# A new issue order in an attention and maxout-FFN kernel, with the loads of later batches as pieces of their own

## The chip, the core and the metric

The kernel runs on one core of one Trainium2 chip. A core has TensorE (PE, matmuls), VectorE (DVE), ScalarE (ACT), GpSimd (POOL) and SyncE (SP), each with an instruction stream of its own that it works off in order, and 16 DMA engines that all streams share. The metric is the device time of one execution in microseconds: before, the median of 3 runs is 178.24 us (178.22 to 178.28).

## The reference

Eight batches, 8 heads, a sequence of 576, head dimension 64, 32 memory slots. `phi` is turned into weights over the sequence, K and V are summed into 32 slots with them, and q attends to the slots. The result, 4608 tokens of 512 values, goes through a feed-forward network whose hidden layer is the maximum of three products.

```python
# _attn_ref (cut)
a = np.exp(phi - np.max(phi, axis=2, keepdims=True))
a = a / (np.sum(a, axis=2, keepdims=True) + 1e-09)
k_m = np.einsum('bhsm,bhsd->bhmd', a, k)
v_m = np.einsum('bhsm,bhsd->bhmd', a, v)
scores = scale * np.matmul(q, k_m.transpose(0, 1, 3, 2))
attn = softmax(scores)              # cut: max, exp, divide by the sum
out = np.matmul(attn, v_m)          # (8, 8, 576, 64)
# reference (cut): tokens x (heads * head_dim) = 4608 x 512
h = np.maximum(np.maximum(x @ w1, x @ w2), x @ w3)     # 512 -> 768
return h @ w_out                                       # 768 -> 512
```

## The kernel before

The kernel never forms `x`. As `attn @ v_m @ w` is `attn @ (v_m @ w)`, it folds the weights into the 32 slots of each head of a batch (D), and takes all hidden values straight from `attn`. It also uses max(a, b, c) = c + max(a - c, b - c, 0): `w1` and `w2` are replaced by their differences to `w3` (V), the relu and the max take the rest, and the part of `w3` goes around the hidden layer as `w3 @ w_out` (W and O).

The work is cut into pieces with one letter each, and the kernel is a list of them; `B@3` is piece B of batch 3. The order in the list is the order on every engine, as the schedule is manual. In the loop `+` and `-` after a name move it to a later or an earlier batch.

| piece | what it does | engines |
|---|---|---|
| E | exp of phi | ACT |
| B | sums of K and V (72 matmuls of 192 columns) | PE |
| N, K | divide by the sum of phi's exps; transpose (to `kvt`) | DVE; PE, then a DVE copy |
| Q0, Q1 | transpose q in 32x32 blocks, half each | DVE |
| S, M, R, X | scores and their exp; sums; reciprocal as exp(-ln); product `attn` | PE, ACT; PE; ACT; DVE |
| W, O, V | transpose w3, w3 @ w_out, differences of the weights (batch 0 alone) | PE, DVE; PE, ACT; DVE |
| D0 to D3 | fold `kvt` into the weights, evacuate to `wp` | PE, then ACT or DVE |
| F0 to F11 | a hidden tile: even ones end in a relu, odd ones in a max | PE, then ACT (even) or DVE (odd) |
| T0 to T4 | an output tile of 128 tokens and its store (T4 only in odd batches) | PE, then ACT or DVE, SP |
| Z24 | 24 matmuls on a zero tile | PE |

The loads are issued on GpSimd's queue. The buffers hold two batches, so the load of a batch needs the buffer of the batch two before it to be free. The first 14 are issued ahead of all pieces; each later one directly behind the last piece that reads its buffer:

```python
inp = ctx.enter_context(tc.tile_pool(name="inp", bufs=2))     # ph, qq
acc_pool = ... name="accp", bufs=3, space=PSUM                # tag "acc": B, S, M, D, F
one_pool = ... name="onep", bufs=2, space=PSUM                # tag "one": Z, W, O, K, T
# ...
load_ph(0)
load_kv(0)
load_q(0)
ident = const.tile([P, P], BF16, name="ident")
make_identity(nc, ident)
load_w(2)
nc.gpsimd.dma_start(out=wo_sb, in_=moe_w_out.rearrange("(t p) c -> p t c", p=P))
load_w(0)
load_w(1)
load_ph(1)
load_kv(1)
load_q(1)
# ...
EVAC = {"D": "aasa", "T": "vaavv"}     # a: ACT, v: DVE, s: half each
# ...
loads = ((load_ph, "E"), (load_kv, "B"), (load_q, "Q0 Q1"))

def done(b, n):
    issued.add((b, n))
    for f, names in loads:
        names = names.split()
        if n in names and b + 2 < B and all((b, m) in issued for m in names):
            f(b + 2)
# ...
issue(0, "Z24")
att_exp(0, halves[0])
att_exp(0, halves[1])
done(0, "E")
att_kv(0, range(0, NP // 2))
issue(0, "Z9")
att_kv(0, range(NP // 2, NP))
done(0, "B")
run(0, "N Z9 K Q0 Q1 S W0 W1 M0 R0 W2 M1 R1 V0")
# ... a list of pieces for batches 0 to 2 and the first ones of batch 3, then:
for b in range(2, B - 1):
    run(b, "T4- F6 F0 F7 F2 F1 F8 F10 F4 F9 F3 T2- S+ B++ N++ D3+ Q0++ E+++ T3- M0+")
    run(b, "R0+ F5 F11 M1+ X0+ R1+ T0 X1+ K++ D2+ D0+ D1+ T1 Q1++")
```

The weights w1, w2, w3 are `load_w(0)`, `load_w(1)`, `load_w(2)`, called w0, w1 and w2 below; `wo` is `moe_w_out`. V0 needs w2 and w0. V1 has two halves, of which the second needs w1; V2 needs w1. D0, D1, D2 need V0, V1, V2. k3 is the load of K of batch 3, and so on.

Of the kernel before, what the change touches and what calls it, by code (L numbers as in the profile page):

```python
# [15 lines left out]
def kernel(  # L16
# [12 lines left out]
    nc = tc.nc  # L29

    B, H, S, D = q.shape
    M = phi.shape[-1]
    P = 128
    NP = H // 2
# [36 lines left out]
    wo_sb = const.tile([P, FT, DM], BF16, name="wo_sb")  # L71
# [5 lines left out]
    def by_pair(src, b):  # L77
        return src[b].rearrange("h s d -> (h s) d").rearrange(
            "(j p c) d -> p j (c d)", p=P, c=NC
        )  # L80

    halves = [slice(0, NP // 2), slice(NP // 2, NP)]
# [11 lines left out]
    def load_kv(b):  # L94
        kv = kvos[b % 2]
        loaded.setdefault(b, {})["kv"] = kv
        for h in halves if b == 0 else [slice(0, NP)]:
            for i, src in enumerate((k, v)):
                nc.gpsimd.dma_start(  # L99
                    out=kv[:, i].rearrange("p j c d -> p j (c d)")[:, h],  # L100
                    in_=by_pair(src, b)[:, h],
                )

    def load_q(b):
        qq = inp.tile([P, NP, NC, D], BF16, name="qq")
        loaded.setdefault(b, {})["q"] = qq
        nc.gpsimd.dma_start(  # L107
            out=qq.rearrange("p j c d -> p j (c d)"), in_=by_pair(q, b)
        )

    def load_w(i):
        w = (moe_w1, moe_w2, moe_w3)[i]
        nc.gpsimd.dma_start(
            out=w_sb[:, :, i], in_=w.rearrange("(j p) f -> p j f", p=P)
        )

    load_ph(0)
    load_kv(0)
    load_q(0)
    ident = const.tile([P, P], BF16, name="ident")  # L120
    make_identity(nc, ident)
    load_w(2)
    nc.gpsimd.dma_start(out=wo_sb, in_=moe_w_out.rearrange("(t p) c -> p t c", p=P))
    load_w(0)
    load_w(1)
    load_ph(1)
# [18 lines left out]
            )  # L145


    EVAC = {"D": "aasa", "T": "vaavv"}

    def evacuate(kind, n, out_, in_):  # L150
        e = EVAC[kind][n]
        if e == "s":
            nc.scalar.copy(out=out_[:, 0], in_=in_[:, 0])
            nc.vector.tensor_copy(out=out_[:, 1], in_=in_[:, 1])
        elif e == "a":
            nc.scalar.copy(out=out_, in_=in_)  # L156
        else:
            nc.vector.tensor_copy(out=out_, in_=in_)  # L158
# [45 lines left out]
    def att_exp(b, js=slice(0, NP)):  # L204
        s = st.setdefault(b, {})
        if "e" not in s:
            s["e"] = work.tile([P, NP, NC, M], BF16, name="e")
        nc.scalar.activation(out=s["e"][:, js], in_=loaded[b]["ph"][:, js], func=AF.Exp)  # L208

    def att_kv(b, js=range(NP)):  # L210
        s = st[b]
        if "kvp" not in s:
            s["kvp"] = acc_pool.tile([P, NG, BANK], FP32, name="kvp", tag="acc")
        kv, kvp = loaded[b]["kv"], s["kvp"]
        for c in range(NC):
            for j in js:
                for a in range(NG):
                    r = slice(HP * a, HP * (a + 1))
                    nc.tensor.matmul(  # L219
                        kvp[M * j : M * (j + 1), a, 0 : 3 * D],  # L220
                        lhsT=s["e"][r, j, c, :],
                        rhs=kv[r, :, j, c, :],
                        start=(c == 0),
                        stop=(c == NC - 1),
                        tile_position=(HP * a, M * j),
                    )

    def att_kv_norm(b):

        s = st[b]  # L230
        kvp = s["kvp"]
        rden = work.tile([P, NG], FP32, name="rden")
        nc.vector.reciprocal(out=rden, in_=kvp[:, :, 2 * D])  # L233
        kvn = work.tile([P, 3, P], BF16, name="kvn")
        nc.vector.tensor_tensor(
            out=kvn[:, 0].rearrange("p (a d) -> p a d", a=NG),
            in0=kvp[:, :, D : 2 * D],
            in1=rden.unsqueeze(2).to_broadcast([P, NG, D]),
            op=ALU.mult,
        )  # L240
        for g in range(NG):
            kn = kvn[:, 1:3, HP * g : HP * (g + 1)]
            nc.vector.tensor_scalar_mul(
                out=kn.rearrange("p h (t d) -> p h t d", t=2),
                in0=kvp[:, g, 0:D]
                .rearrange("p (h d) -> p h d", h=2)
                .unsqueeze(2)
                .to_broadcast([P, 2, 2, R]),
                scalar1=rden[:, g : g + 1],
            )  # L250
        s["kvn"] = kvn

    def att_kv_t(b):


        s = st[b]
        ps = one_pool.tile([P, 3, P], BF16, name="kvtp", tag="one")
        for n in range(3):
            nc.tensor.transpose(ps[:, n], s["kvn"][:, n], ident)
        kvt = work.tile([P, 3, P], BF16, name="kvt")  # L260
        nc.vector.tensor_copy(out=kvt, in_=ps)
        s["kvt"] = kvt

    def att_q(b, n):


        s = st.setdefault(b, {})
        if "qT" not in s:
            s["qT"] = work.tile([P, NP, NC, 2, R], BF16, name="qT")
        j = halves[n]  # L270
        nc.vector.transpose(  # L271
            out=s["qT"][:, j].rearrange("p j c h r -> p (j c h r)"),
            in_=loaded[b]["q"][:, j].rearrange("p j c d -> p (j c d)"),
        )
# [34 lines left out]
    def att_sum(b, g):  # L309
        s = st[b]  # L310
        e2 = s["e2"]
        sm = acc_pool.tile([P, 2, BANK], FP32, name="sm", tag="acc")
        for h in range(2):
            nc.tensor.matmul(  # L314
                sm[:, h, 0:SH],
                lhsT=blkones,
                rhs=e2[:, g, h * SH : (h + 1) * SH],
                start=True,
                stop=True,
            )  # L320
        s["sm", g] = sm
# [126 lines left out]
            nc.sync.dma_start(out=rows[:, h[1]], in_=ot[:, h[1]])  # L448


    issued = set()
    loads = ((load_ph, "E"), (load_kv, "B"), (load_q, "Q0 Q1"))

    def issue(b, n):

        if not 0 <= b < B or (n == "T4" and b % 2 == 0):
            return
        i = int(n[1:]) if len(n) > 1 else None
        {
            "E": lambda: att_exp(b),  # L460
            "B": lambda: att_kv(b),
            "N": lambda: att_kv_norm(b),
            "K": lambda: att_kv_t(b),
            "Q": lambda: att_q(b, i),
            "S": lambda: att_score(b),
            "M": lambda: att_sum(b, i),
            "R": lambda: att_rec(b, i),
            "X": lambda: att_mul(b, i),
            "D": lambda: fold(b, i),
            "F": lambda: ffn1(b, i),  # L470
            "T": lambda: ffn2(b, i),
            "W": lambda: w3_t(i),
            "O": lambda: w3_o(i),
            "V": lambda: w_diff(i),
            "Z": lambda: warm_up(i),
        }[n[0]]()
        done(b, n)

    def done(b, n):
        issued.add((b, n))  # L480
        for f, names in loads:
            names = names.split()
            if n in names and b + 2 < B and all((b, m) in issued for m in names):
                f(b + 2)

    def run(b, text):

        for w in text.split():
            issue(b + w.count("+") - w.count("-"), w.rstrip("+-"))

    issue(0, "Z24")
    att_exp(0, halves[0])
    att_exp(0, halves[1])
    done(0, "E")
    att_kv(0, range(0, NP // 2))
    issue(0, "Z9")
    att_kv(0, range(NP // 2, NP))
    done(0, "B")
    run(0, "N Z9 K Q0 Q1 S W0 W1 M0 R0 W2 M1 R1 V0")
    for w in """  # L500
        O2@0 X1@0 O1@0 X0@0 O3@0 D0@0 O0@0 V1@0 F6@0 F0@0 V2@0 F2@0 D1@0 D2@0 F1@0 F4@0 F7@0
        F3@0 E@1 F5@0 F10@0 F8@0 F11@0 B@1 N@1 D3@0 F9@0 K@1 D0@1 Q0@1 E@2 Q1@1 T3@0 D2@1
        S@1 T1@0 M0@1 M1@1 T0@0 R1@1 R0@1 D3@1 X1@1 D1@1 X0@1 B@2 N@2 T2@0 F2@1 F6@1 F8@1
        Q0@2 Q1@2 F7@1 F0@1 K@2 F3@1 E@3 F1@1 F9@1 F4@1 F10@1 S@2 F5@1 F11@1 M1@2 B@3 R1@2
        D3@2 N@3 T0@1 Q0@3 X1@2 M0@2 E@4 R0@2 T1@1 D1@2 D0@2 D2@2 X0@2 Q1@3 K@3
    """.split():
        n, b = w.split("@")
        issue(int(b), n)
    for b in range(2, B - 1):
        run(b, "T4- F6 F0 F7 F2 F1 F8 F10 F4 F9 F3 T2- S+ B++ N++ D3+ Q0++ E+++ T3- M0+")  # L510
        run(b, "R0+ F5 F11 M1+ X0+ R1+ T0 X1+ K++ D2+ D0+ D1+ T1 Q1++")
    run(B - 1, "T4- F6 T2- F10 F2 F7 F8 F11 F0 F4 F1 F5 F9 F3 T3- T0 T4 T2 T3")
    ffn2(B - 1, 1, last=True)


# [28 lines left out]
```

The softmax here doesn't subtract the row's maximum and nothing guards it: scores larger than these inputs give would overflow.

## Time and profile before

| | before |
|---|---|
| time, median of 3 | 178.24 us |
| span of the profiled execution | 177.6 us |
| PE busy | 159.8 us |
| ACT busy, DVE busy | 105.9 us, 104.5 us |
| bytes read from HBM, written | 39.32 MB, 9.44 MB |
| loads on GpSimd's queue, issue to landing | 16 to 21 us (medians by tensor, from batch 1 on and the weights) |
| F, T, D on PE: matmuls | 384, 216 + 64 + 16, 256 |

Busy time counts the time in which an engine has an instruction in work, and PE's matmuls are pipelined, so a busy PE is not PE at its peak. The page has the span in 40 equal slices, with the busy share of each engine in tenths; it tells in which stage an engine is full. The chain of work that ended last names, from the end backwards, what each step waited for. "Issue to landing" is the time from a load's issue on GpSimd to its completion, and holds its time in the queue as well. Lines in the profile are lines of the kernel: L99 the loads of K and V, L107 those of q, L92 those of phi, L219 B, L358 D, L383 the matmuls of F, L393 and L395 its relu and max, L411, L420 and L429 the matmuls of T, L271 Q, L338 X, L191 V.

### The profile page before, as it was taken

To read this page: it belongs to the slowest core of one execution; us is meant where nothing else is said; L and a number is where in the kernel's file an instruction comes from. 1 tells how busy PE (TensorE), PEld (TensorE's weight loads), DVE (VectorE), ACT (ScalarE), POOL (GpSimd) and SP (SyncE) were. 2 spreads that over 40 slices of the span, in tenths; PEclk is the share of its full clock that TensorE was granted. 3 is DMA by queue.
4 is the path that set the end of the run, shared out by engine and by line. 5 is a ranking of instruction groups with operands and counts; after the bars stand their busy time and mean duration, and the time that the engine had idled before them with its cause. 6 is when DMAs were issued, how large, how long until landed. Compare 5 with 4: busy or idle time off the path is not lost.

```text
span 177.6 us, 4447 instructions
## 1 busy us (share of the span) xinstructions
PE 159.8 (90%) x1914; PEld 89.0 (50%) x1914; DVE 104.5 (59%) x164; ACT 105.9 (60%) x158; POOL 28.3 (16%) x43
## 2 busy tenths in 40 slices
PE   7895897788996596999999999999999999999990
PEld 2352634453564342755565547456664565466440
DVE  6407418679379366749855965597479553717420
ACT  4100467857885686659867767679477558872010
POOL 7951112043133050104013010000000000000000
PEclk9999699999999999999999999999999999999999
DMA  5999999999999999999999999213013201330333
GB/s 154 160 206 209 207 210 275 208 261 222 236 320 237 275 208 241 289 235 298 235 260 277 230 270 188 98 59 118 0 63 122 111 9 69 114 118 0 122 118 120
DMA packets 21973, 31.76 MB, mean 179 GB/s; under 512 B 1216, under 2 KB 16576, under 8 KB 21952
## 3 DMA queue, kind: packets, MB, share of 16 engines
q0 software_dynamic: 16080, 21.43, 63.4%
q1 hardware_dynamic: 5728, 9.90, 15.7%
q8 instruction: 15, 0.25, 0.5%
q10 hardware_dynamic: 144, 0.13, 0.2%
q14 instruction: 6, 0.05, 0.1%
HBM read 39.32 MB, written 9.44 MB: 275 GB/s over the span
## 4 chain that ended last, share of the span: by engine, by line
PE 64%; DMA 23%; ACT 4%; POOL 3%; issue 2%; DVE 2%; ACTq 0%; DVEq 0%; POOLq 0%
PE po L411 23%; PE acc L383 22%; DMA kvo<-in_v_dram 12%; DMA w_sb<-in_moe_w_dram 11%; PE po L420 7%; PE wps L358 4%; PE kvp L219 3%; POOL kvo L99 2%; ACT h L393 2%; PE sm L314 2%; ACT wp L156 1%; PE sc L293 1%; PE po L429 1%; PE po L175 1%; DVE w_sb L191 1%
## 5 line engine op out<-in xcount | busy, mean ns | idle before, releaser
L383 PE MATMUL acc<-attn,wp 128*128 128x288 bf16 x384 | 51.9, 286 | 4.0 <-DVE attn L338 1.6
L411 PE MATMUL po<-wo_sb,hT 128*128 128x512 bf16 x216 | 52.6, 380 | 0.0
L395 DVE TENSOR_TENSOR hT<-acc,h 128x576 bf16<-128x576 f32 x48 | 34.6, 752 | 20.4 <-PE acc L383 17.8
L383 PEld LDWEIGHTS <-wp 128*128 128x128 bf16 x384 | 37.0, 97 | 18.2 <-issue 6.5
L393 ACT ACTIVATE h<-acc 128x576 bf16<-128x576 f32 x48 | 28.9, 655 | 12.7 <-PE acc L383 12.7
L411 PEld LDWEIGHTS <-hT 128*128 128x128 bf16 x216 | 19.8, 97 | 24.4 <-issue 4.3
L156 ACT CAST wp<-wps 128x1024 bf16<-128x1024 f32 x24 | 23.7, 1019 | 4.9 <-PE wps L358 4.9
L158 DVE COPY ot<-po 128x512 f32<-128x512 f32 x20 | 13.6, 681 | 16.7 <-PE po L420 13.3
L271 DVE STREAM_TRANSPOSE qT<-qq 128x1152 bf16<-128x1152 bf16 x16 | 21.6, 1364 | 1.7 <-DMA qq<-in_q_dram 1.7
L156 ACT COPY ot<-po 128x512 f32<-128x512 f32 x15 | 9.0, 597 | 20.7 <-PE po L420 20.7
L420 PE MATMUL po<-wp,attn 128*128 128x512 bf16 x64 | 19.0, 379 | 0.0
L302 ACT ACTIVATE e<-sc 128x576 bf16<-128x576 f32 x16 | 9.6, 654 | 14.1 <-PE sc L293 14.1
L143 PE MATMUL po<-warm 128*128 128x512 bf16 x42 | 11.3, 427 | 1.2 <-DVE warm L131 1.2
L327 ACT ACTIVATE ln<-sm 128x576 f32<-128x576 f32 x16 | 10.3, 643 | 2.8 <-PE sm L314 2.8
L338 DVE TENSOR_TENSOR attn<-e,r 128x576 bf16<-128x576 bf16 x16 | 11.8, 747 | 0.0
L99 POOL DMA_DIRECT2D kvo<-in_k_dram x9 | 6.7, 747 | 29.9 <-PE kvp L219 17.5
L333 ACT ACTIVATE r<-ln 128x576 f32<-128x576 f32 x16 | 10.9, 683 | 0.5
L208 ACT ACTIVATE e<-ph 128x1152 bf16<-128x1152 f32 (+1 forms) x9 | 9.5, 1058 | 2.6 <-DMA ph<-in_phi_dram 2.4
L233 DVE RECIPROCAL rden<-kvp 128x2 f32<-128x2 f32 x8 | 1.4, 170 | 16.3 <-PE kvp L219 16.3
L219 PE MATMUL kvp<-kvo,e 64*32 64x192 bf16 x576 | 8.4, 244 | 2.7 <-DMA kvo<-in_v_dram 2.7
L107 POOL DMA_DIRECT2D qq<-in_q_dram x8 | 6.0, 745 | 28.4 <-DVE qT L271 16.5
L420 PEld LDWEIGHTS <-attn 128*128 128x128 bf16 x64 | 6.2, 98 | 7.0
(43 smaller groups left out, 113.2 us busy)
## 6 DMA issues: line engine op xcount, KB each, us to landing
out_dram<-ot SPq DMA_DIRECT2D x35, 256.0 KB, 3.0
qq<-in_q_dram POOLq DMA_DIRECT2D x8, 576.0 KB, 18.7
ph<-in_phi_dram POOLq DMA_DIRECT2D x7, 576.0 KB, 20.5
kvo<-in_k_dram POOLq DMA_DIRECT2D x7, 576.0 KB, 19.1
kvo<-in_v_dram POOLq DMA_DIRECT2D x7, 576.0 KB, 20.8
w_sb<-in_moe_w_dram POOLq DMA_DIRECT2D x3, 768.0 KB, 19.2
wo_sb<-in_moe_w_out_dram POOLq DMA_DIRECT2D x1, 768.0 KB, 16.3
ph<-in_phi_dram SPq DMA_DIRECT2D x2, 288.0 KB, 2.9
```

Source lines behind the costliest of these rows:

```text
L143: nc.tensor.matmul(po[:, 0:BANK], lhsT=warm[:, 0:P], rhs=warm, start=True, stop=True)
L156: nc.scalar.copy(out=out_, in_=in_)
L158: nc.vector.tensor_copy(out=out_, in_=in_)
L219: nc.tensor.matmul(kvp[M * j : M * (j + 1), a, 0 : 3 * D], lhsT=s["e"][r, j, c, :], rhs=kv[r, :, j, c, :], start=(c == 0), stop=(c == NC - 1),
L271: nc.vector.transpose(out=s["qT"][:, j].rearrange("p j c h r -> p (j c h r)"), in_=loaded[b]["q"][:, j].rearrange("p j c d -> p (j c d)"),)
L333: nc.scalar.activation(out=r, in_=ln, func=AF.Exp, scale=-1.0)
L338: nc.vector.tensor_tensor(out=attns[b // 2][:, g, (b % 2) * S : (b % 2 + 1) * S], in0=s["e2"][:, g, 0:S], in1=s["r", g], op=ALU.mult,)
L383: nc.tensor.matmul(acc[:, h, 0:SH], lhsT=wps[b][:, g, w * DF + ft * P : w * DF + (ft + 1) * P], rhs=attn[:, g, c0 : c0 + SH], start=(g == ...
L393: nc.scalar.activation(out=h1, in_=a, func=AF.Relu)
L395: nc.vector.tensor_tensor(out=hT[:, ft, (b % 2) * S : (b % 2 + 1) * S].rearrange("p (h n) -> p h n", h=2), in0=a, in1=s["h1", ft], op=ALU.max,
L411: nc.tensor.matmul(po, lhsT=hT[:, fc, c0 : c0 + P], rhs=wo_sb[:, fc, :], start=(fc == 0), stop=False,)
L420: nc.tensor.matmul(po, lhsT=attn[:, g, c0 : c0 + P], rhs=wp3s[b][:, g, :], start=False, stop=(g == NG - 1),)
```

## The change

Loads become pieces of the list: L0, L1, L2 are the loads of phi, of K and V, and of q. They may then stand anywhere behind the last reader of their buffer. All pieces are put in a new order, which was made with a longer delay of those loads in mind. On the way, w3 and w_out are issued ahead of the identity, the split evacuation moves from D2 to D1, T4 is evacuated by ACT, the warm-up of Z24, Z9, Z9 becomes Z26, Z5, Z18, and K comes last in the loop. No computation is added or removed beyond the warm-up matmuls.

```diff
--- before.py
+++ after.py
@@ -117,10 +117,10 @@
     load_ph(0)
     load_kv(0)
     load_q(0)
+    load_w(2)
+    nc.gpsimd.dma_start(out=wo_sb, in_=moe_w_out.rearrange("(t p) c -> p t c", p=P))
     ident = const.tile([P, P], BF16, name="ident")
     make_identity(nc, ident)
-    load_w(2)
-    nc.gpsimd.dma_start(out=wo_sb, in_=moe_w_out.rearrange("(t p) c -> p t c", p=P))
     load_w(0)
     load_w(1)
     load_ph(1)
@@ -145,7 +145,7 @@
             )
 
 
-    EVAC = {"D": "aasa", "T": "vaavv"}
+    EVAC = {"D": "asaa", "T": "vaava"}
 
     def evacuate(kind, n, out_, in_):
         e = EVAC[kind][n]
@@ -448,17 +448,15 @@
             nc.sync.dma_start(out=rows[:, h[1]], in_=ot[:, h[1]])
 
 
-    issued = set()
-    loads = ((load_ph, "E"), (load_kv, "B"), (load_q, "Q0 Q1"))
-
     def issue(b, n):
 
         if not 0 <= b < B or (n == "T4" and b % 2 == 0):
             return
         i = int(n[1:]) if len(n) > 1 else None
         {
-            "E": lambda: att_exp(b),
-            "B": lambda: att_kv(b),
+            "L": lambda: (load_ph, load_kv, load_q)[i](b),
+            "E": lambda: [att_exp(b, h) for h in (halves if b == 0 else [slice(0, NP)])],
+            "B": lambda: [att_kv(b, range(NP)[h]) for h in (halves if b == 0 else [slice(0, NP)])],
             "N": lambda: att_kv_norm(b),
             "K": lambda: att_kv_t(b),
             "Q": lambda: att_q(b, i),
@@ -474,42 +472,28 @@
             "V": lambda: w_diff(i),
             "Z": lambda: warm_up(i),
         }[n[0]]()
-        done(b, n)
-
-    def done(b, n):
-        issued.add((b, n))
-        for f, names in loads:
-            names = names.split()
-            if n in names and b + 2 < B and all((b, m) in issued for m in names):
-                f(b + 2)
 
     def run(b, text):
 
         for w in text.split():
             issue(b + w.count("+") - w.count("-"), w.rstrip("+-"))
 
-    issue(0, "Z24")
-    att_exp(0, halves[0])
-    att_exp(0, halves[1])
-    done(0, "E")
-    att_kv(0, range(0, NP // 2))
-    issue(0, "Z9")
-    att_kv(0, range(NP // 2, NP))
-    done(0, "B")
-    run(0, "N Z9 K Q0 Q1 S W0 W1 M0 R0 W2 M1 R1 V0")
     for w in """
-        O2@0 X1@0 O1@0 X0@0 O3@0 D0@0 O0@0 V1@0 F6@0 F0@0 V2@0 F2@0 D1@0 D2@0 F1@0 F4@0 F7@0
-        F3@0 E@1 F5@0 F10@0 F8@0 F11@0 B@1 N@1 D3@0 F9@0 K@1 D0@1 Q0@1 E@2 Q1@1 T3@0 D2@1
-        S@1 T1@0 M0@1 M1@1 T0@0 R1@1 R0@1 D3@1 X1@1 D1@1 X0@1 B@2 N@2 T2@0 F2@1 F6@1 F8@1
-        Q0@2 Q1@2 F7@1 F0@1 K@2 F3@1 E@3 F1@1 F9@1 F4@1 F10@1 S@2 F5@1 F11@1 M1@2 B@3 R1@2
-        D3@2 N@3 T0@1 Q0@3 X1@2 M0@2 E@4 R0@2 T1@1 D1@2 D0@2 D2@2 X0@2 Q1@3 K@3
+        E@0 L0@2 Z26@0 B@0 N@0 Z5@0 K@0 Q0@0 Q1@0 L2@2 L1@2 Z18@0 W1@0 W0@0 S@0 M0@0 R0@0
+        W2@0 M1@0 O1@0 O0@0 V0@0 R1@0 O3@0 X0@0 X1@0 D0@0 V2@0 O2@0 F6@0 F2@0 F4@0 V1@0 F0@0
+        D2@0 D1@0 F7@0 F3@0 E@1 L0@3 F8@0 F1@0 F9@0 F5@0 F10@0 F11@0 B@1 L1@3 D3@0 N@1 K@1
+        D0@1 Q1@1 Q0@1 L2@3 D2@1 D1@1 T2@0 S@1 T0@0 E@2 L0@4 M0@1 R0@1 M1@1 X0@1 R1@1 X1@1
+        T3@0 T1@0 Q1@2 F0@1 F8@1 F1@1 F9@1 F6@1 F2@1 D3@1 B@2 L1@4 Q0@2 L2@4 F4@1 N@2 F7@1
+        K@2 F10@1 F3@1 S@2 F5@1 F11@1 M1@2 E@3 L0@5 M0@2 R1@2 R0@2 T0@1 D0@2 X0@2 D2@2 B@3
+        L1@5 N@3 X1@2 T1@1 D1@2 D3@2 Q0@3 Q1@3 L2@5 K@3 E@4 L0@6
     """.split():
         n, b = w.split("@")
         issue(int(b), n)
     for b in range(2, B - 1):
-        run(b, "T4- F6 F0 F7 F2 F1 F8 F10 F4 F9 F3 T2- S+ B++ N++ D3+ Q0++ E+++ T3- M0+")
-        run(b, "R0+ F5 F11 M1+ X0+ R1+ T0 X1+ K++ D2+ D0+ D1+ T1 Q1++")
-    run(B - 1, "T4- F6 T2- F10 F2 F7 F8 F11 F0 F4 F1 F5 F9 F3 T3- T0 T4 T2 T3")
+        run(b, "F6 F0 T4- F7 F4 F1 F2 F10 F3 F8 F5 F9 T2- S+ Q0++ B++ L1++++ D3+ E+++")
+        run(b, "L0+++++ N++ T3- M0+ R0+ M1+ F11 X0+ T0 R1+ X1+ Q1++ L2++++ D0+ D2+ D1+")
+        run(b, "T1 K++")
+    run(B - 1, "T4- F0 F2 F1 F10 F8 F11 F3 T3- F4 F6 F5 F7 F9 T2- T2 T3 T4 T0")
     ffn2(B - 1, 1, last=True)
```

## The prediction

> **What bounds the kernel now.** I read the page first, then the busy time by stage, then the chain of work that ended last, and last the waits of single engines. First the page, in 40 slices of 4.44 us:
>
> ```profile
> PE 159.8 (90%) x1914; PEld 89.0 (50%) x1914; DVE 104.5 (59%) x164; ACT 105.9 (60%) x158; POOL 28.3 (16%) x43
> ...
> PE   7895897788996596999999999999999999999990
> ...
> DMA  5999999999999999999999999213013201330333
> ```
>
> TensorE (PE) is full from the 18th slice to the end, and has holes only before it. The DMA engines are full from the second slice to about 110 us, also in the second half, where PE waits for nothing. So two regimes: up to 76 us PE waits for something, after it PE alone is the bound. Busy time by stage (the columns are length; busy and count of PE, PEld, DVE, ACT, POOL; clock; DMA share; GB/s):
>
> ```profile
> 50.00:55.00 5.00, 3.83 (x31) 2.72 (x30) 3.76 (x6) 3.42 (x7) 0.95 (x2) 1.00 1.14 286
> ...
> 60.00:65.00 5.00, 3.62 (x93) 2.14 (x94) 2.29 (x7) 3.50 (x5) 1.51 (x3) 1.00 1.19 219
> ...
> 80.00:85.00 5.00, 5.00 (x38) 2.79 (x44) 4.59 (x8) 4.32 (x6) 1.85 (x3) 1.00 1.14 291
> ```
>
> Summing 5.00 minus PE busy from 25 to 75 us: 0.98 + 1.09 + 0.62 + 0.57 + 0 + 1.17 + 0.69 + 1.38 + 0.77 + 1.07 = 8.3 us of idle PE. From 75 to 170 us it is 0. **These 8.3 us are all that an order can win** after the weights have landed. Who ended them, from the waits of PE between 25 and 78 us (us in total, times, longest):
>
> ```profile
> PE kvp L219 <- DMA kvo<-in_v_dram: 1.6, 1, 1.6
> PE wps L358 <- DVE w_sb L191: 1.6, 2, 1.0
> PE acc L383 <- DVE attn L338: 1.6, 1, 1.6
> PE acc L383 <- DVE hT L395: 1.3, 1, 1.3
> ```
>
> The first is B@3, K and V sums of batch 3, which stands in PE's queue before its V is there. The chain of work shows it (start, us, what):
>
> ```profile
> 7.06 19.20 DMA w_sb<-in_moe_w_dram
> ...
> 39.56 21.68 DMA kvo<-in_v_dram
> 61.25 0.14 issue
> 61.38 0.94 PE kvp L219 x72
> ```
>
> And VectorE's timeline shows the q of batches 2 and 3 missing in the same way; the brackets give the wait before:
>
> ```profile
> 51.82 2.64 DVE L271 STREAM_TRANSPOSE qT<-qq 128x1152 bf16<-128x1152 bf16 x2 [1.24 <-DMA qq<-in_q_dram]
> ...
> 65.55 1.38 DVE L271 STREAM_TRANSPOSE qT<-qq 128x1152 bf16<-128x1152 bf16 x1 [0.46 <-DMA qq<-in_q_dram]
> ```
>
> The first of them is behind the 1.3 us too: the max of F that PE waits for at 55.16 us stands behind this transpose on VectorE.
>
> Issue time plus time to landing of each load gives the arrivals (us): v1 37.4, q1 40.3, ph2 41.7, k2 44.5, v2 47.3, q2 51.8, ph3 54.8, k3 58.4, v3 61.3, ph4 62.7, q3 65.6, k4 68.3, v4 72.7, q4 75.5, v5 84.2, q5 89.0, v7 108.3, q7 113.1. They come one after the other, about 3 us for each load of 1.18 MB of HBM bytes, and wait some 20 us in the queue: a delay of 19 to 25 us at issue is queue, not distance. B@2 ran at 47.97 and B@3 at 61.38, each at the moment of arrival; B@4 ran at 78.34, 5.6 us after v4, and the slack grows from there.
>
> **What the Trainium skill says.** "DMA: Bandwidth & Descriptors", section "Queues, rings and completion order": on each DMA engine descriptors are consumed in ring order. The arrivals above agree: they come in order of issue. The same page, "Anatomy of one DMA — SWDGE (gpsimd) path": DMA engines do not wait on semaphores, the issuing sequencer does before dispatch. So a load that waits for its buffer holds up every load behind it on GpSimd; the trace agrees (GpSimd stood 4.57 us at 35.85 us for the exp of batch 1, with K, V behind it). [...]w2, wo, w0 and w1, 1.57 MB of f32 each, landed at 18.7, 22.5, 26.3 and 30.0 us here, 3.8 us apart or some 415 GB/s on the read side[...]. "TensorE: Matmul & The Clock Gate", "What's actually happening": an idle window lowers the clock. Here the clock was 0.83 between 15 and 25 us. The longer warm-up Z18 may keep it up there, but that stage ends on a DMA, so I give it nothing.
>
> **The change part by part.**
>
> *Loads.* Their number, sizes and buffers stay. On GpSimd's queue q2 moves ahead of k2 and v2, q3 ahead of ph4, and the same later for q5 and ph6. The queue never runs dry before 110 us, so bytes ahead of a load decide: q2 arrives near 44.5 instead of 51.8, v2 near 51.5 instead of 47.3, q3 near 64.2 instead of 65.6, ph4 near 65.6; v3, v4 and q4 stay at 61.3, 72.7 and 75.5. w2 and wo are issued 0.5 us sooner, ahead of the identity (0.22 + 0.29 us), but stand behind q0 in a full queue: no gain. w0 and w1 (26.3 and 30.0 us) do not move.
>
> *Evacuations.* D1 is split between ScalarE and VectorE instead of D2: same work. T4 goes to ScalarE: four times 0.60 us there for 0.68 us on VectorE. Both engines are at 60%: nothing.
>
> *Order.* PE's pieces, as the chain shows them: F 0.51 us, T 1.29 + 0.43 = 1.72, T4 1.84, S 0.40, B 0.87, D 0.26, M 0.24, O 1.42. I walk the new order by hand with these, 0.65 us for an activation, 1.02 for a whole evacuation of D, 0.72 for a max of F, 1.31 for one transpose of q, 1.1 for N, and three PSUM buffers.
> - To 33 us: Z18 ends at 19.6 (0.236 us a matmul), then W1 W0 S M0 W2 M1 to 24.1, O1 O0 O3 D0 O2 after the w3T copies, so F@0 starts at about 30.5 (before: 29.3). V2 now stands ahead of V1 and waits for w1 until 30.0; V1 ends at 32.5, just before D1 needs it at 32.9. D1's two halves are out at 35.5, F3 goes there, seven F end at about 38.8: B@1 at 38.9 instead of 37.56, **1.3 us late**.
> - 39 to 51: N, K, kvt stand directly after one another (PE idle some 1.4 us), D0 D2 D1 T2, S at 44.2 behind the two transposes, T0, then E@2 (1.17 us) between the exps and R0 on ScalarE, so X1 ends at 50.8. F@1 starts at 50.85 (before: 50.56, with B@2 and D3@1 already done, another 1.1 us). **Behind by 1.4 us.**
> - 51 to 62.7: here before lost its 1.3 and 1.6 us. Now six F stand ahead of B@2, which runs at about 54.2, after v2. q2 is long there. N@2, S@2, M1@2 cost PE some 2.5 us of small waits. M0@2, T0@1, D0@2 and D2@2 (0.24 + 1.72 + 0.52 = 2.5 us) now stand ahead of B@3, which starts at 62.65, 1.3 us after v3: no wait for DMA.
> - 62.7 to F@2: T1@1, D1, D3, K@3, then F6 F0 at 66.05 when X1@2 is out, T4@1, and F7@2 at 68.9. Before had finished the same pieces (T4@1, F6, F0) at 70.82 + 2 x 0.51 = 71.85. Before then waited another 0.25 us. **Gain so far 71.85 - 68.9 + 0.25 = 3.2 us.**
> - From there both are PE without holes, and the pieces are the same. B@4 falls at about 75.6, v4 lands at 72.7: 3 us to spare. Q0@4 now stands ahead of B@4 on VectorE at about 75.6 against q4 at 75.5: just there. The end (0.38 us copy, output, 4.1 us from the last matmul to the span's end) stays.
>
> Hand-overs between engines that I left out, some ten of 0.05 to 0.1 us on the path, cost about 0.6 us. Sum: 3.2 - 0.6 = 2.6 us, and 178.24 - 2.6 = **175.6 us**, 1.5% faster.
>
> **The rivals.** (1) *The waits only move.* My walk has 1.4 us lost near 40 us, and small waits of 2.5 us near 56 us. If these are longer, the gain is nothing: 178 us. For it: the in-order queues of ScalarE and VectorE, which are 0.74 and 0.70 busy in 35 to 50 us. Against: before had the same kind of waits. (2) *All waits go.* If the order fits better than I see, PE keeps only the wait for V, about 3 of the 8.3 us: 178.24 - 5.3 = 173 us. For it: the order was made for a delay, which is what before lacked. Against: what I found at 33 and 40 us. (3) *DMA becomes the bound.* PE comes 3 us sooner to B@4 and Q0@4, which had 5.6 us and more of slack to their data. If outputs push q4 by 2 us, VectorE stands there, N@4 and F11@2's max behind it, and T0@2: 177.5 us. (4) *The later loop is no longer without holes*, as F11 stands alone between M1 and X0, and K comes last. With 0.3 us in each of five batches the gain falls to 1.1 us: 177.1. Against: the ScalarE and VectorE work of a batch, about 12 us each of 17.2 (27.9 and 27.7 us busy in 100 to 140 us), is the same.
>
> **Range and chances.** Centre 175.6. The walk is no better than 1.5 to 2 us: rivals 1, 3 and 4 give the upper end, 178.0, rival 2 the lower, 173.2. The line of 2% is 174.7, 0.9 us below the centre: faster by over 2% 0.33, within 2% 0.63, slower by over 2% 0.04, as nothing in it costs 3.6 us.
>
> **What would show it.** Right: no wait of PE for V at B@3, no wait of VectorE for q2; B@3 near 62.6; F7@2 near 69; PE at 5.00 of 5.00 from 70 us on; idle of PE in 25 to 75 us near 5.5 instead of 8.3 us. Wrong: a wait of Q0@4 for q4, holes in PE after 80 us, or F@1 starting after 52 us.

## The result, and the profile after

The changed kernel takes **176.3 us** (median of 4 runs, 175.89 to 177.35) where the kernel before takes 178.26 in the same session: a ratio of 0.9895 with a 95% interval of 0.9847 to 0.9943. A second set of five runs, in another session, gave 176.67 against 178.35, 0.9902 (0.9881 to 0.9922). So the gain is 1.7 to 2.0 us, some 1%. The prediction was 175.6 us (range 173.2 to 178.0), a gain of 2.6 us: the measured times lie 0.7 to 1.1 us above its centre.

The same rows of the page as before, now for the changed kernel (busy time by engine; then PE and DMA in tenths in 40 slices of 4.39 us):

```profile
PE 162.1 (92%) x1921; PEld 89.1 (51%) x1921; DVE 103.9 (59%) x160; ACT 108.0 (62%) x162; POOL 28.3 (16%) x43
...
PE   7959599797999998999999999999999999999990
...
DMA  5999999999999999999999999312013201311333
```

Before, PE's 13th, 14th and 16th slice were 6, 5 and 6; they are 9, 9 and 8 now, and of the slices behind the 10th all others but the last are full. The DMA row is nearly what it was. Busy time by stage of the changed kernel (length; busy and count of PE, PEld, DVE, ACT, POOL; clock; DMA share; GB/s):

```profile
50.00:55.00 5.00, 4.87 (x108) 3.54 (x107) 5.00 (x6) 3.44 (x6) 0.00 (x0) 1.00 1.16 257
...
60.00:65.00 5.00, 5.00 (x106) 2.65 (x105) 3.18 (x8) 4.80 (x7) 2.00 (x3) 1.00 1.16 267
65.00:70.00 5.00, 4.43 (x43) 2.08 (x42) 3.91 (x5) 4.44 (x7) 0.31 (x2) 1.00 1.18 238
...
80.00:85.00 5.00, 5.00 (x50) 2.27 (x48) 4.35 (x6) 4.72 (x8) 0.76 (x1) 1.00 1.15 259
```

The two stages that held the waits for data, 50 to 55 and 60 to 65 us, had 3.83 and 3.62 us of busy PE and have 4.87 and 5.00. What is left is in 65 to 70 us. PE's timeline of the changed kernel shows both (start, length, what; the bracket is the wait ahead of it):

```profile
62.50 0.93 PE L219 MATMUL kvp<-kvo,e 64*32 64x192 bf16 x72
...
67.15 0.65 PE L383 MATMUL acc<-attn,wp 128*128 128x288 bf16 x4 [0.57 <-DVE wp L154]
```

B@3 starts without a wait: v3 landed at 60.3 us. The 0.57 us are the first F of batch 2 that needs D1@2 (F0), which waits for the half of it that VectorE evacuates.

**A second pair of profiles.** The profiled executions above ran some 1 us longer than the medians (179.35 before, 177.35 after). A second profile of each kernel comes from runs of 178.40 and 176.19 us, with spans of 176.6 and 174.4; these two are compared below. The longest waits of PE between 25 and 78 us (total, times, longest), of the kernel before:

```profile
PE wps L358 <- DVE w_sb L191: 1.7, 2, 1.0
PE acc L383 <- DVE attn L338: 1.6, 1, 1.6
PE acc L383 <- DVE hT L395: 1.2, 1, 1.2
PE kvp L219 <- DMA kvo<-in_v_dram: 0.9, 1, 0.9
PE wps L358 <- DVE kvt L261: 0.6, 1, 0.6
```

and of the changed one:

```profile
PE wps L358 <- DVE w_sb L191: 1.8, 2, 1.0
PE acc L383 <- DVE wp L154: 0.9, 2, 0.6
PE wps L358 <- DVE kvt L261: 0.5, 1, 0.5
```

The waits for v3 (0.9), for F's max behind the transposes of q2 (1.2) and for `attn` (1.6) are gone, and one of 0.6 us for `wp` has come. The wait for the weights at the start (1.7) has stayed.

The wait for `attn` was not one for late data. VectorE's timeline of the kernel before, then of the changed one:

```profile
68.36 0.69 DVE L154 CAST wp<-wps 128x512 bf16<-128x512 f32 x1 [1.74 <-ACT wp L153]
68.97 0.75 DVE L338 TENSOR_TENSOR attn<-e,r 128x576 bf16<-128x576 bf16 x1
```

```profile
63.56 0.75 DVE L338 TENSOR_TENSOR attn<-e,r 128x576 bf16<-128x576 bf16 x1
65.27 0.69 DVE L154 CAST wp<-wps 128x512 bf16<-128x512 f32 x1 [0.96 <-ACT wp L153]
```

Before, X1@2 stands on VectorE behind its half of D2@2, and that half waits 1.74 us for ScalarE's half. In the new order X1@2 stands ahead of the split D1@2. So the lead grows in steps. Up to F@1 nothing is won, and the moves at the start (w3 and w_out earlier, another warm-up) gained nothing: F@0 starts at 29.11 us before and 29.12 now, F@1 at 50.51 and 49.34, where before has also done B@2 and D3@1 (1.1 us). At T4@1 (67.66 and 67.89) the changed kernel has F6 and F0 (1.02 us) behind it already and leads by 0.8 us. Only then does the kernel before wait 1.58 us for `attn` and 0.25 us for a relu, and the lead is 2.66 us at 70 us. No run moves X1@2 alone, so its share is read from the traces.

### The profile page after: what moved, and what is told of

Read it like the earlier page. It is cut to its first block, busy times and chain, and to the rows that moved or that the text cites. A ratio compares the mean times of both kernels' runs of the same rounds, so it can differ in the third digit from the quotient of the medians.

```text
span 175.5 us, 4464 instructions
## 1 busy us (share of the span) xinstructions
PE 162.1 (92%) x1921; PEld 89.1 (51%) x1921; DVE 103.9 (59%) x160; ACT 108.0 (62%) x162; POOL 28.3 (16%) x43
## 4 chain that ended last, share of the span: by engine, by line
PE 73%; ACT 9%; DMA 8%; DVE 4%; POOL 2%; issue 1%; DVEq 0%; POOLq 0%
PE acc L383 25%; PE po L411 24%; DMA w_sb<-in_moe_w_dram 8%; PE po L420 7%; PE wps L358 4%; PE kvp L219 3%; PE sm L314 2%; ACT wp L156 2%; PE po L175 2%; POOL kvo L99 1%; PE sc L293 1%; ACT h L393 1%; DVE hT L395 1%; PE po L429 1%; ACT r L333 1%
## 5 line engine op out<-in xcount | busy, mean ns | idle before, releaser
L383 PE MATMUL acc<-attn,wp 128*128 128x288 bf16 x384 | 52.6, 286 | 2.1 <-ACT wp L156 0.9
L395 DVE TENSOR_TENSOR hT<-acc,h 128x576 bf16<-128x576 f32 x48 | 35.1, 754 | 18.0 <-PE acc L383 12.2
L383 PEld LDWEIGHTS <-wp 128*128 128x128 bf16 x384 | 36.5, 97 | 16.2 <-issue 2.5
L393 ACT ACTIVATE h<-acc 128x576 bf16<-128x576 f32 x48 | 29.4, 652 | 12.8 <-PE acc L383 11.9
L156 ACT COPY ot<-po 128x512 f32<-128x512 f32 x19 | 11.3, 596 | 21.2 <-PE po L420 15.7
L158 DVE COPY ot<-po 128x512 f32<-128x512 f32 x16 | 11.1, 692 | 20.2 <-PE po L420 20.2
L143 PE MATMUL po<-warm 128*128 128x512 bf16 x49 | 12.7, 419 | 1.2 <-DVE warm L131 1.2
L219 PEld LDWEIGHTS <-e 64*32 64x32 bf16 x576 | 7.1, 90 | 4.1 <-issue 4.0
```

The source lines that it names most:

```text
L143: nc.tensor.matmul(po[:, 0:BANK], lhsT=warm[:, 0:P], rhs=warm, start=True, stop=True)
L219: nc.tensor.matmul(kvp[M * j : M * (j + 1), a, 0 : 3 * D], lhsT=s["e"][r, j, c, :], rhs=kv[r, :, j, c, :], start=(c == 0), stop=(c == NC - 1),
L383: nc.tensor.matmul(acc[:, h, 0:SH], lhsT=wps[b][:, g, w * DF + ft * P : w * DF + (ft + 1) * P], rhs=attn[:, g, c0 : c0 + SH], start=(g == ...
L393: nc.scalar.activation(out=h1, in_=a, func=AF.Relu)
L395: nc.vector.tensor_tensor(out=hT[:, ft, (b % 2) * S : (b % 2 + 1) * S].rearrange("p (h n) -> p h n", h=2), in0=a, in1=s["h1", ft], op=ALU.max,
```

## The experiments

All ratios are to the kernel before, measured beside it on the same chip.

**1. The loads at their old places, in the new order of pieces.** From the changed kernel; pieces L are taken out, and each load is issued behind the last reader of its buffer again. On GpSimd's queue this only exchanges q2 with k2 and v2 early on.

```diff
-        E@0 L0@2 Z26@0 B@0 ... Q1@0 L2@2 L1@2 Z18@0 ...      (and all other L)
+        E@0 Z26@0 B@0 ... Q1@0 Z18@0 ...
+        issued.add((b, n))
+        for f, names in loads: ...                            # as in the kernel before
```

> The changed kernel with each later load issued by the last reader of its buffer again, as before. On GpSimd this exchanges only q2 with k2 and v2; all other loads keep their order. Theory (the gain is the order of the pieces, the loads' own places are worth next to nothing): q2 lands near 51.5 us, the first transpose of q of batch 2, which stood at 51.1 us, waits under 0.5 us, v2 lands near 47.5; time within 0.5 us of the changed kernel, 176 to 176.8. Rival (q's early arrival is what won the time): the 1.3 us wait of F behind VectorE comes back, time near 177.5.

177.08 us, 0.9949 (0.9932 to 0.9967): the interval doesn't meet that of the second set of the changed kernel (0.9881 to 0.9922), but it overlaps that of the first (0.9847 to 0.9943). VectorE's timeline of this run, then PE's:

```profile
50.86 1.38 DVE L271 STREAM_TRANSPOSE qT<-qq 128x1152 bf16<-128x1152 bf16 x1 [0.83 <-DMA qq<-in_q_dram]
```

```profile
52.93 0.65 PE L383 MATMUL acc<-attn,wp 128*128 128x288 bf16 x4 [1.04 <-DVE hT L395]
```

The wait for q2 is back, the next max of F stands behind it, and PE waits 1.04 us, against 1.21 us in the kernel before. F@1 started at 49.28 us (second profile of the changed kernel: 49.34), B@3 at 62.21 (61.37): 0.8 us lost in between. So the loads' own places are worth 0.4 us (by the medians) to 0.8 us (by this trace and the ratios), and the new order of pieces, with the loads where they were, still gains 0.9 us by this ratio.

**2. The new order of loads, with the old pieces.** From the kernel before; a load is held back until it is its turn in the new order.

```diff
+    order = [(f, c) for c in range(2, B) for f in (load_ph, load_kv, load_q)]
+    order[1], order[2] = order[2], order[1]
-                f(b + 2)
+                ready.add((f, b + 2))
+        while order and order[0] in ready: ...                # issue in this order
```

> The kernel before with the loads of later batches in the order of the changed kernel (q2 ahead of k2 and v2, q3 ahead of ph4, q5 ahead of ph6), all pieces as before. Theory: v2 lands near 51.3 instead of 47.3, and B@2, which stands at 47.97 in PE's queue, waits 3 us or more; VectorE's wait for q2 (1.24 us) and what follows from it goes; net 1 to 2.5 us slower than before, 179.2 to 180.8. Rival (the order of the loads alone is a gain): 176.5 to 177.5.

181.43 us, 1.0155 (1.0107 to 1.0203): slower than before by 2.8 us (1.9 to 3.6), more than the 1 to 2.5 expected. PE's timeline of this run, then its stage from 50 us:

```profile
51.04 0.94 PE L219 MATMUL kvp<-kvo,e 64*32 64x192 bf16 x72 [3.20 <-DMA kvo<-in_v_dram]
51.91 2.72 PE L411 MATMUL po<-wo_sb,hT 128*128 128x512 bf16 x6
```

```profile
50.00:55.00 5.00, 3.96 (x80) 1.93 (x81) 2.91 (x6) 0.04 (x1) 1.48 (x2) 0.70 1.16 280
```

B@2 now stands ahead of v2 as B@3 did ahead of v3, and the six matmuls after the 3.2 us took 2.72 us instead of 1.46: PE's clock was 0.70 of full speed in 50 to 55 us. Moving q2's load forward took its place from k2 and v2, and here it paid only where B@2, which needs v2, had been moved back as well.

**3. A warm start.** From the changed kernel; nine warm-up matmuls between the halves of B@0, and 24 for the 18 ahead of the transposes of w3.

```diff
+   ... warm_up(9) between the two halves of B@0
-   ... Q1@0 L2@2 L1@2 Z18@0 W1@0 ...
+   ... Q1@0 L2@2 L1@2 Z24@0 W1@0 ...
```

> The changed kernel with nine more warm-up matmuls between the two halves of B@0 (as before had) and Z24 in place of Z18, so that PE has no hole of over 1 us up to the transposes of w3. Theory (the half clock from 21.8 to 25 us, behind the holes at 10 and 18 us, costs the w3 products 0.8 us and the runs their spread): the clock stays at 1.00, F@0 starts near 29.4 instead of 30.25, F3@0 near 34.8 instead of 35.4, and the time is 175.6 to 175.9 with runs within 0.4 us of one another. Rival (the stage ends on the arrival of w1 anyway, and the spread is from elsewhere): 176.3 and the same spread.

176.79 us, 0.9923 (0.9893 to 0.9952): nothing gained. The clock was 1.00 from 15 to 25 us, but V0's wait for w0 comes last either way: F@0 started at 28.64 instead of 29.12 us with w0 landing 0.7 us sooner in this run (V0 at 25.49 instead of 26.20). B@3 started at 60.87 instead of 61.37, and there its last matmul waited. PE's timeline:

```profile
62.37 0.25 PE L219 MATMUL kvp<-kvo,e 64*32 64x192 bf16 x1 [0.58 <-issue]
```

The profile names no releaser for this wait. It was not v3, which had landed at 60.27 us (issue 39.37, landing 20.9 us later). What this run had won at 28 us was gone at 62, to a gap whose cause stays open.

**4. B@3 and N@3 later, in the kernel before.** The simplest remedy for its longest wait.

```diff
-  ... M1@2 B@3 R1@2 D3@2 N@3 T0@1 Q0@3 X1@2 M0@2 E@4 R0@2 T1@1 D1@2 ...
+  ... M1@2 R1@2 D3@2 T0@1 Q0@3 X1@2 M0@2 E@4 R0@2 T1@1 B@3 N@3 D1@2 ...
```

> The kernel before with one piece moved: B@3 and its N@3 go behind T1@1, so that PE has T0@1, M0@2 and T1@1 in hand while V of batch 3 is on its way. Theory: the wait of 1.65 us for V at 59.7 us goes, PE waits there some 0.7 us for the last max of F@1 instead, and the time falls by 0.7 to 1.5 us, to 176.8 to 177.5. Rival (the wait only moves to the attn of batch 2): within 0.3 us of before.

179.83 us, 1.0074 (1.0047 to 1.0101): slower, by 0.7% to judge from the ratio. The 17 runs lie in two groups: six at 178.4 to 178.7, close to the kernel before, and eleven at 179.5 to 180.8, the profiled one (179.68) among them. The wait for v3 went, and another came. VectorE's timeline of this run, then PE's, and its stage from 65 us:

```profile
64.08 1.38 DVE L271 STREAM_TRANSPOSE qT<-qq 128x1152 bf16<-128x1152 bf16 x1 [1.56 <-DMA qq<-in_q_dram]
...
66.43 0.60 DVE L243 TENSOR_SCALAR kvn<-kvp,rden 128x128 bf16<-128x128 f32 x2
```

```profile
67.08 0.41 PE L358 MATMUL wps<-w_sb,kvt 64*32 64x512 bf16 x8 [2.02 <-DVE kvn L243]
...
67.60 2.12 PE L411 MATMUL po<-wo_sb,hT 128*128 128x512 bf16 x6
```

```profile
65.00:70.00 5.00, 2.98 (x27) 1.06 (x21) 3.81 (x9) 2.43 (x3) 1.46 (x2) 0.82 1.16 251
```

N@3 now stands behind Q0@3 on VectorE, which waits 1.56 us for q3; B@3's PSUM buffer is not free until N@3 has read it, and the next piece, D1@2, needs that buffer. After the 2 us the clock was down again (0.82 in 65 to 70 us). Moved by itself, B@3 gained nothing here: the pieces on the other engines that depend on it did not come along.

**5. The changed kernel again, timed closely.** No edit.

> The changed kernel once more, beside the next three on one chip, to narrow its interval. Ratio to before 0.987 to 0.992. The run-to-run spread, 1.5 us in its first runs, is there again if it comes from the half clock at 20 to 25 us.

176.67 us, as told above; the five runs lie within 0.6 us.

**6. A tighter start.** Experiment 3, and V1 ahead of V2, D1 ahead of D2, F7 of batch 0 later, its F10 and F11 behind B@1, to start B@1 sooner.

```diff
-  ... D0@0 V2@0 O2@0 F6@0 F2@0 F4@0 V1@0 F0@0 D2@0 D1@0 F7@0 F3@0 E@1 L0@3 F8@0 ... F10@0 F11@0 B@1 ...
+  ... D0@0 V1@0 O2@0 F6@0 F2@0 F4@0 V2@0 F0@0 D1@0 D2@0 F3@0 F8@0 F1@0 E@1 L0@3 ... B@1 ... F10@0 F11@0 ...
```

> The warm start of the earlier run, and three moves in batch 0: V1 ahead of V2 and D1 ahead of D2 (so that the difference that needs no w1 is not held up), and F10@0, F11@0 behind B@1, where PE stood 1.1 us for N@1 and K@1. Theory (the start gains, but B@2 and B@3 then reach the front of PE's queue at the arrival of v2 near 51 and v3 near 61, so DMA is the bound again): PE starts F@1 near 48 instead of 50.5, the wait for V at B@3 comes back with 0.5 to 2 us, and the time is 0.3 to 1.3 us under the changed kernel. Rival (DMA has slack; PE alone was late): all 2.5 us come through, 173.8.

176.96 us, 0.9927 (0.9909 to 0.9946): nothing gained. PE's timeline:

```profile
37.39 0.94 PE L219 MATMUL kvp<-kvo,e 64*32 64x192 bf16 x72 [0.77 <-DMA kvo<-in_v_dram]
```

B@1 reached the arrival of v1, 37.3 us, and waited; F@1 started at 49.52, no sooner than without it (49.34). My expectation of about 48 failed: I had taken B@1's place for the limit, and it is v1's arrival and the work behind it. The wait for v3 that I expected at B@3 did not come either: v3 landed at 60.9 us, B@3 started at 61.55, and only its last matmul stood 0.34 us, with no releaser named, as in experiment 3.

**7. More work ahead of B@3, and the old loop.** Experiment 6, and T1@1 and X1@2 ahead of B@3, K@3 behind F6@2, and the loop of the kernel before.

```diff
-  ... D2@2 B@3 L1@5 N@3 X1@2 T1@1 D1@2 D3@2 Q0@3 Q1@3 L2@5 K@3 ...
+  ... D2@2 X1@2 T1@1 B@3 L1@5 N@3 D1@2 D3@2 Q0@3 Q1@3 L2@5 ...
```

> The tight start, and in addition T1@1 and X1@2 ahead of B@3 and N@3, K@3 behind F6@2, the first transpose of q behind N in the loop and the loop's order of before. Theory (what wins against a late V is work in front of it, if N does not stand behind a wait for q): B@3 has no wait over 0.3 us, F7@2 starts near 67.5 instead of 69.6, time 173.8 to 174.8, 1.5 to 2.5 us under the changed kernel. Rival (waits move again, as when B@3 alone was moved): within 0.5 us of the tight start.

177.29 us, 0.9942 (0.9922 to 0.9962): 0.6 us above the changed kernel in the same session, where I expected 1.5 to 2.5 us below it. There is no wait for v3 here either (B@3 starts at 63.36), but another one, PE's timeline:

```profile
65.44 0.67 PE L383 MATMUL acc<-attn,wp 128*128 128x288 bf16 x4 [0.71 <-DVE kvn L243]
```

Again PSUM: F0@2 waits for N@3 to release a buffer, as N@3 comes later with B@3.

**8. The changed kernel with the old loop, last batch and evacuations.** Only the start is new.

```diff
-    EVAC = {"D": "asaa", "T": "vaava"}
+    EVAC = {"D": "aasa", "T": "vaavv"}
-        run(b, "F6 F0 T4- F7 F4 F1 F2 F10 F3 F8 F5 F9 T2- S+ Q0++ B++ L1++++ D3+ E+++") ...
+        run(b, "T4- F6 F0 F7 F2 F1 F8 F10 F4 F9 F3 T2- S+ B++ L1++++ N++ D3+ Q0++ E+++ L0+++++ T3- M0+") ...
-    run(B - 1, "T4- F0 F2 F1 F10 F8 F11 F3 T3- F4 F6 F5 F7 F9 T2- T2 T3 T4 T0")
+    run(B - 1, "T4- F6 T2- F10 F2 F7 F8 F11 F0 F4 F1 F5 F9 F3 T3- T0 T4 T2 T3")
```

> The changed kernel with the loop, the last batch and the evacuations of before, loads at their places there. Theory (two batches of the new loop take 34.49 us on the chain, of the old one 34.35; the new F6, F0 ahead of T4 space their matmuls by their evacuation): 0.2 to 0.5 us faster than the changed kernel. Rival (the loop's new order is part of the gain): slower by 0.3 us or more.

**175.90 us** (175.76 to 177.77), 0.9888 (0.9851 to 0.9926): the lowest median of all, 0.8 us under the changed kernel in the same session, though the intervals overlap. PE's timeline:

```profile
65.16 1.46 PE L411 MATMUL po<-wo_sb,hT 128*128 128x512 bf16 x6
66.55 0.62 PE L429 MATMUL po<-wp,attn 128*64 128x512 bf16 x4
67.10 5.26 PE L383 MATMUL acc<-attn,wp 128*128 128x288 bf16 x40
```

F runs without the 0.57 us wait: PE is busy for 9.71 of 10.00 us in 60 to 70 instead of 9.43 in the second profile of the changed kernel. Two edits can do it, and no run parts them. T4@1 stands ahead of F6 and F0 of batch 2, which gives D's evacuation 2 us more. And D1 is not split any more: ScalarE starts it whole at 64.57 us, and as such an evacuation takes 1.02 us it is out at about 65.6 (an estimate), where the two halves, one behind the other, were out at 65.96. The spans of the two profiles differ by 0.4 us (174.0, 174.4).

**9 and 10. No q of batches 2 and 3.** In the kernel before and in the changed one, the loads of q2 and q3 are left out; batches 2 and 3 use the q of 0 and 1. These kernels leave out 2.4 MB of reads, and their outputs of batches 2 and 3 are another computation's. k, v and phi land sooner as well. Nothing in PE's work changes.

```diff
+        if b in (2, 3):
+            loaded.setdefault(b, {})["q"] = loaded[b - 2]["q"]
+            return
```

> The kernel before without the loads of q of batches 2 and 3; their pieces use the q of batches 0 and 1, so the outputs of those batches are others, and all else is the same. It takes 2.4 MB out of the DMA queue ahead of v3. Theory (before lost its time to data that came late for the places it was used at): VectorE's wait for q2 goes, v3 lands near 58 and B@3 has no wait; 1.3 us and 1.6 us of PE's waits go, the time falls by 2.3 to 3.5 us, to 174.8 to 176. Rival (the other engines' order holds it up as much): under 1 us.

> The changed kernel without the same two loads of q. Theory (the changed order no longer waits for any load after batch 1): v2 lands near 48 and v3 near 55, both far ahead of their use, and the time stays within 0.5 us of the changed kernel, 176.2 to 176.8. Rival (it is still held up by DMA somewhere between 40 and 76 us): 1 us faster or more.

Before without them: 177.24 us, 0.9951 (0.9933 to 0.9969), 0.9 us of gain. The changed kernel without them: 176.55, 0.9902 (0.9872 to 0.9932), just what it is with them. So earlier loads of batches 2 and 3 gain the changed kernel nothing any more, and they did gain the kernel before something. PE's timeline of experiment 9 (its lines of code stand three lower):

```profile
58.19 0.94 PE L222 MATMUL kvp<-kvo,e 64*32 64x192 bf16 x72 [0.37 <-DVE hT L398]
...
67.63 2.61 PE L386 MATMUL acc<-attn,wp 128*128 128x288 bf16 x20 [1.59 <-DVE attn L341]
```

B@3 starts 2.2 us sooner than in the second profile of before, and F@2 at 67.63 instead of 69.87: 2.24 us. That I expected 2.3 to 3.5 us of time and measured 0.9 is a miss: of the 2.24 us, this trace gave 0.6 back by 137 us (with one gap of 0.38 us at 112.6 that PE had without a named releaser) and 0.4 after the last matmul. Why, I haven't found. The wait of 1.59 us for `attn` is as long as before: it isn't the data's, but that of X1@2's place on VectorE behind its half of D2@2, which waits 2.29 us for ScalarE's half in this run.

**11. w_out last among the weights.** Experiment 8, with w_out loaded behind w1, O spread over the F of batch 0, V1 ahead of V2, and X1@2 and T1@1 ahead of B@3 with K@3 behind T4@1.

```diff
     load_w(1)
+    nc.gpsimd.dma_start(out=wo_sb, ...)                     # was ahead of the identity
-  ... M1@0 O1@0 O0@0 V0@0 R1@0 O3@0 X0@0 X1@0 D0@0 V2@0 O2@0 F6@0 ...
+  ... M1@0 Z6@0 R1@0 V0@0 X0@0 X1@0 D0@0 V1@0 F6@0 ... O1@0 F9@0 F5@0 O0@0 O3@0 B@1 L1@3 N@1 O2@0 ...
```

> The changed kernel with the old loop (T4 ahead of F6 and F0), w_out loaded behind w1 instead of ahead of w0, the four products w3 @ w_out moved into and behind F@0, and T1@1 ahead of B@3. Theory (up to 37 us the arrivals of w0, w1 and v1 pace PE, and w_out is the one that can wait): w0 lands near 22.5, w1 near 26.3, F@0 starts near 25.5, PE reaches B@1 at v1's arrival near 37.4 with F11, D3 and one product still in hand to cover N@1 and K@1, F@1 starts 0.5 to 1.5 us sooner than 49.3, and the time is 174.5 to 175.5. Rival (PE's work up to v3 was already dense, the loads only change places): 175.9, as with the old loop alone.

176.29 us, 0.9892 (0.9857 to 0.9926): no better than experiment 8. PE's timeline:

```profile
26.23 2.13 PE L383 MATMUL acc<-attn,wp 128*128 128x288 bf16 x16 [1.14 <-ACT wp L156]
...
30.17 3.30 PE L383 MATMUL acc<-attn,wp 128*128 128x288 bf16 x20 [1.04 <-ACT wp L156]
```

F@0 starts 2.9 us sooner than in the changed kernel (26.23, 29.12), between two waits of 1.14 and 1.04 us for the evacuations of D; O's matmuls come after it, and B@1 is at 38.26, F@1 at 51.16 us (37.85 and 49.34 there). The work only changed places.

**12. The kernel before, profiled again.** No edit; to have a profile of it near its median.

> The kernel before once more, for a second trace: the first one's run took 179.35 us, 1.1 us over the median of 178.26, as the first trace of the changed kernel stood 0.9 us over its median. Theory (the first trace had a late start by DMA arrivals, the waits behind it are the same): F@0 starts near 28.6 instead of 29.3, the waits for q2 and v3 are there again with 2 to 3 us together, the span is near 176.5. Rival (the waits of 40 to 62 us themselves are shorter in a usual run): they sum to under 1.5 us.

178.39 us, 1.0001 (0.9981 to 1.0021). Its PE timeline has the three waits that the change is about, and their sizes in a usual run:

```profile
54.99 2.24 PE L383 MATMUL acc<-attn,wp 128*128 128x288 bf16 x16 [1.21 <-DVE hT L395]
...
60.43 0.94 PE L219 MATMUL kvp<-kvo,e 64*32 64x192 bf16 x72 [0.86 <-DMA kvo<-in_v_dram]
...
69.87 2.61 PE L383 MATMUL acc<-attn,wp 128*128 128x288 bf16 x20 [1.58 <-DVE attn L338]
```

The first two, which are late data, make 2.1 us. F@0 started at 29.11, half a us later than one theory had it.

## Why the prediction was right, and where it was off

**What bounds the kernel: right, but for one wait.** Until 70 us PE waits, from then on it is full. The two waits for data (1.21 and 0.86 us) went with the change, and with q2 and q3 left out, and v3 sooner, the changed kernel gains nothing more (experiment 10). But the wait of 1.58 us for `attn`, as long in the prediction's list as that for v3, was not told apart from these: it comes from the order on VectorE and stays when the data are early (experiment 9). And the prediction has B@2 run at the arrival of v2; it ran at 47.97 without a wait, 0.6 us after v2 (47.3). Only B@3 waited.

**Loads: right.** Arrivals by issue plus landing in the changed kernel, predicted and found in the first profile (us): q2 44.5, 44.7; v2 51.5, 51.2; v3 61.3, 60.3; q3 64.2, 63.7; ph4 65.6, 65.1; v4 72.7, 72.1; q4 75.5, 75.8. The Trainium skill states in "DMA: Bandwidth & Descriptors", section "Queues, rings and completion order", that each DMA engine takes descriptors in ring order, in a paragraph on the queues of SyncE and ScalarE; the seven loads here, on GpSimd's queue, landed in their order of issue too. That order, with 3 us for each load of 1.18 MB ahead, placed each to 1 us. "Next to nothing" for their own places, which I wrote ahead of experiment 1, was wrong: the exchange of q2 with k2 and v2 is worth 0.4 to 0.8 us, as VectorE's queue carries q2's lateness on to PE.

**The walk: right to 0.4 us up to B@3.** Predicted, then first and second profile: F@0 30.5, 30.25 and 29.12; B@1 38.9, 38.98 and 37.85; F@1 50.85, 50.48 and 49.34; B@3 62.65, 62.50 and 61.37. The second profile is 1.1 us ahead all along. One error did not show, by luck: Z18 ended at 18.0 us in the first profile and not at 19.6, but the transposes of w3 behind it waited for w2 until 19.31.

**"Z18 may keep the clock up, but that stage ends on a DMA": right, and nearly whole.** In the first profile the clock was down to 0.50 for 3.2 us from 21.8 us on, over O, whose first 18 matmuls took 4.87 us instead of the 4.04 of the second profile. Yet D0@0 started at once when V0 had its w0: V0 at 26.90 and D0 at 28.18 in the first profile, 26.20 and 27.48 in the second, where PE waited 1.03 us for it. So 0.7 of the 1.1 us between the two profiles is the arrival of w0; the slow O, whose evacuations on ScalarE stand ahead of D0's, leaves at most 0.4. The Trainium skill ("TensorE: Matmul & The Clock Gate", "What's actually happening") has half the rate after an idle window of about 3.4 us; here holes of 1.95 us at 10 and 1.30 us at 18 us stood ahead of it.

**F7@2 at 68.9: the term that was short, by 0.7 us.** It was 69.58 in the first profile. My walk gave F0@2 its start when X1@2 was out, and forgot that D1@2 had just been split and its VectorE half comes last: the 0.57 us wait. "D1 is split ... instead of D2: same work" was right as to work and wrong as to time: VectorE's half waits for ScalarE's, and the two took from 64.64 to 65.96 us, 1.3 us, in the second profile, where a whole evacuation on ScalarE takes 1.02. Experiment 8, with T4@1 ahead of F6 and F0 and D1 whole, does not have this wait. The gain up to there was thus not 3.2 but 71.85 - 69.58 + 0.25 = 2.5 us.

**"From there both are PE without holes, and the pieces are the same": wrong by 0.4 to 0.5 us.** PE is at 5.00 of 5.00 from 70 us on, as said. Yet from one T4 to that of two batches later the changed kernel needs 34.50 us in the second profile (67.89 to 102.39, to 136.89), the kernel before 34.34 (103.95 to 138.29). Counted where both have finished the same pieces (T4, F6 and F0 of the pair of batches), the lead is 2.66 us at 70 us (70.85 + 0.25 of wait that before still had, less 68.44), 2.42 at 138 us (139.86 less 137.44) and 2.2 at the end of the span. Rival 4 had this at up to 0.3 us a batch; it is under 0.1. It isn't the loop's order alone: with the old loop, experiment 8 took 34.44 and 34.64 us for the same two pairs. What costs it stays open; no wait shows in it.

**The sum.** 3.2 less 0.6 for hand-overs was 2.6. The profiles have 2.5 (first pair) and 2.66 (second) at 70 us with all hand-overs in it, less 0.4 to 0.5 from there on: spans 2.1 and 2.2 us apart, and medians 1.7 and 2.0. That 2.6 met the lead at 70 us was luck in part: up to B@3 the walk needed no allowance for hand-overs (62.65 against 62.50 us), and the 0.6 us stood in for the wait that it had forgotten.

**The other rivals.** Rival 1 (the waits only move) is what happened to other moves: experiments 2, 4, 6, 7 and 11 are all of this kind. The change escaped it by moving T0@1, D, M0 and F together with B and the loads. Rival 2 (all waits go) failed at 30 to 50 us, where the weights and v1 set the pace. Rival 3 was half there: Q0@4 waited 0.62 us for q4 (0.73 in the second profile), but PE had enough before it, and did not wait.

**Idle PE.** Predicted 5.5 us in 25 to 75 us, against 8.3; the first profile has 3.7, where O at half clock counts as busy, and the second 4.5, against 7.5 in that of before. So 4.6 and 3.0 us less idle time went with spans 2.1 and 2.2 us shorter: both times the sum overstates the gain.

What stays open: how the 1.7 to 2.0 us divide between late data and the order around X1@2 and D. With early data alone, the kernel before gains 2.24 us at 70 us in the trace and 0.9 us in the times (experiment 9), and still waits for `attn`. And whether experiment 8 truly beats the changed kernel, as its interval overlaps.

## What to carry to other kernels

With the load queue full, the arrival of a load here was set by the loads ahead of it, 3 us for each, so write down the arrivals and set each consumer behind its own, on every engine whose queue it stands in. Move a late consumer together with the pieces that free its buffers and with the load order: here each of these alone was slower (1.5% for the loads, 0.7% for the consumer), and together they won 1%. And walk the evacuation of the last operand as well: the wait that the walk forgot was that of a split copy whose second half starts only behind the first, and the longest single wait of the kernel before stood behind such a half too.

## What the hardware showed that I had not expected

Holes of 2 to 3 us cost more than their length here. After PE waited 3.20 us (experiment 2) and 2.02 us (experiment 4), its clock was 0.70 and 0.82 of full speed in the 5 us stage around it, and six matmuls took 2.72 and 2.12 us instead of 1.46. In the changed kernel's start, holes of 1.95 and 1.30 us stood ahead of a half clock over O in one profile, and holes of 1.82 and 0.96 us ahead of none there in the other. The weights themselves landed up to 1.4 us apart from run to run: V0 started at 25.49, 26.20 and 26.90 us in three profiles with the same loads ahead of it. And a split evacuation did not run in parallel: where VectorE was free, its half waited for ScalarE's, 0.96 us in the changed kernel and 1.74 us in the kernel before.
